# Local attention on other quarters of the array: scores with a head on each half of the partitions, values on all four quarters

## The chip, the cores and the metric

One core of a Trainium2 chip runs the whole program. The metric is the device time of one execution in microseconds (us). Engines are named as in the profile: PE is TensorE's matrix products, PEld its weight loads, DVE is VectorE, ACT is ScalarE, POOL is GpSimd, SP is SyncE, which issues the DMAs here.

## The reference, cut to what matters

```python
def sm_attn(qq, kk, vv):                          # softmax attention
    s = scale * np.matmul(qq, kk.transpose(0, 1, 3, 2))
    s = s - np.max(s, axis=-1, keepdims=True)
    a = np.exp(s)
    a = a / (np.sum(a, axis=-1, keepdims=True) + 1e-09)
    return np.matmul(a, vv)
q_d, k_d, v_d = means of q, k, v over groups of 4 tokens
out_up = np.repeat(sm_attn(q_d, k_d, v_d), 4, axis=2)
mask = np.abs(pos[:, None] - pos[None, :]) < 4    # local attention, 7 keys wide
out_local = softmax attention over the masked scores
x = (out_up + out_local)                          # (4608 tokens, 512)
h = x @ w_in                                      # 512 -> 2048
g = np.where(h >= 1, h, np.where(h <= -1, 0, (h + 1) ** 2 / 4))
return g @ w_out                                  # 2048 -> 512, float32
```

Here q, k and v are 8 batches x 8 heads x 576 tokens x 64 numbers, float32.

## The kernel before, in words

Two heads make a pair: with 64 numbers a head, a pair fills the 128 partitions, head h on the half that begins at 64 h. There are 32 pairs (8 batches of 4), and each goes through `attention` in ten pieces. The attention's output goes into a ring of two batches (`xh`, `xl`: two float32r parts whose sum is the number), and the feed-forward takes 12 chunks of 384 tokens from it, in steps of 128 hidden columns: `mm1` (L387, tile h_ps, then L398 to L404) and `mm2` (L425, tile o_ps).

Local attention cuts the 576 tokens into ten windows of 64 tokens, numbered i = 0 to 9, and computes 64 x 64 scores in each. A product with 64 rows and 64 columns of weights takes a quarter of TensorE's 128 x 128 array. Which quarter is set by its operands: the half of the partitions that they lie on is the row half, and the half of the partitions that the output lies on is the column half. I write a quarter as (row half, column half).

- **Scores (L146, tile sl_ps, 20 products a pair).** Operands are on the half of head h. Windows go two to a group, i = 2g + r, and the output is on half r, in PSUM bank h. For each g the products go to quarters (0,0), (1,1), (1,0), (0,1): all four in turn.
- **Softmax (L163 to L194)** works along a row, over a tile `sl` of 128 x 640. L163 adds the band mask and copies from PSUM to `sl`, through a view with the dimensions h, g, column.
- **Transposes (L213, tile tl_ps, 5 a pair)** of 128 x 128 each: after them (`al`, L217) the partitions are head and key, the columns are window half r and query.
- **Products with the values (L240, tile pl_ps, 20 a pair).** For window i and head h both operands lie on half h, and so does the output: quarters (0,0) and (1,1) alone, in turn. A product's columns are 53 to 61 output tokens. Output goes to PSUM bank 0 for windows 0 to 4 and bank 1 for 5 to 9, for either head.

Every one of these products is in float32, and shows as two passes in the trace: two weight loads and two matmuls, so a pair's 20 products are 40 matmul rows.

Beside these stand the pooled attention (sp_ps L156, tp_ps L222, pp_ps L252) and the sum of both (x, L263).

What sets the order: a scheduler places the instructions from the order in which the program gives them; each engine then runs its own list in that order. The first twelve pairs' pieces and the conversion of the weights from float64 (L298 to L309, on ACT, DVE and POOL) are placed by two written lists (`BEFORE_STEPS`, `FIRST_STEPS`). From the 49th step of the feed-forward on, `attn_step` spreads a pair over four steps, in pieces of 6, 0, 2 and 2, and `mm2` comes two steps behind `mm1`.

Of the kernel before, what the change touches and what calls it, by code (L numbers as in the profile page):

```python
# [17 lines left out]
P = 128  # L18
B, H, S, D = 8, 8, 576, 64
NPAIR = H // 2  # L20
# [12 lines left out]
RING = 2 * S  # L33
# Local attention runs on ten windows of 64 tokens: window start, first output
# token, number of output tokens.
WIN = 64
WIN_START = [0, 58, 116, 174, 232, 285, 343, 401, 459, 512]
OUT_START = [0, 61, 119, 177, 235, 288, 346, 404, 462, 520]
OUT_LEN = [61, 58, 58, 58, 53, 58, 58, 58, 58, 56]
NB = len(WIN_START)  # L40
NG = NB // 2
QB = 48
NQB = SD // QB
KB = 72
NKB = SD // KB
MASKED = -1.0e30
# Products at the very start, on operands that need no load, that take TensorE out of
# its slow clock.
WARM = 10
# The order in which the start's work is given to the scheduler, before the steps of the  # L50
# feed-forward and among the first of them. qN and v: loads of the first batch's
# operands, aN: the next of pair N's ten pieces, w: loads of the next weights, c: the
# conversion of the next unit of weights, s: the next step's product with w_in and its
# activation, m: the next step's product with w_out.
BEFORE_STEPS = """
# [14 lines left out]
class Rotation:  # L70
    """Tiles from several pools in turn."""

# [8 lines left out]
def attention_then_ffn(ctx: ExitStack, tc, qT, kT, vw, vp, band, w_in, w_out, out):  # L81
    nc = tc.nc
# [21 lines left out]
    def load(n, name):  # L104
        """The operand `name` of pair n, into the place that pair n - 1 has read."""
        if n == len(pairs):
            return
        b, p = pairs[n]
        if name == "q" or name == "k":
            t = apool.tile([P, S], F32, name=f"{name}_sb", tag=name, bufs=1)  # L110
            nc.sync.dma_start(t, (qT if name == "q" else kT)[b, p])
        elif name == "vp":
            t = apool.tile([KB, NKB, FACTOR, P], F32, name="vp_sb", tag="vp", bufs=1)
            nc.sync.dma_start(t, vp[b, p].rearrange("k (n f c) -> k n f c", n=NKB, f=FACTOR))
        else:
            t = apool.tile([P, NB, D], F32, name="v_sb", tag="v", bufs=1)
            nc.sync.dma_start(t, vw[b, p].rearrange("k (n d) -> k n d", n=NB))
        loaded[name] = t
# [4 lines left out]
    def attention(n, pool_1, pool_2):  # L123
        """One pair of heads, in ten pieces."""
        b, p = pairs[n]
        q, k = qk[p] if b == 0 else (loaded["q"], loaded["k"])
        M = 2 * QB
        # Sums over the groups of four tokens; the means' factors go into the
        # exponent's scale and into the output's.
        qd = apool.tile([P, SD], F32, name="qd", tag="qd", bufs=1)  # L130
# [8 lines left out]
        yield  # L139
        # Scores.  # L140
        sl_ps = pool_2.tile([P, 2, 512], F32, name="sl_ps", tag="a2")
        for g in range(NG):
            for r, h in ((0, 0), (1, 1), (0, 1), (1, 0)):
                w = WIN_START[2 * g + r]
                hs = slice(h * D, (h + 1) * D)
                nc.tensor.matmul(  # L146
                    sl_ps[r * WIN : (r + 1) * WIN, h, g * WIN : (g + 1) * WIN],
                    q[hs, w : w + WIN],
                    k[hs, w : w + WIN],
                    start=True,  # L150
                    stop=True,
                )
        sp_ps = pool_1.tile([P, 512], F32, name="sp_ps", tag="a1")
# [3 lines left out]
        if n + 1 >= NPAIR:  # L157
            load(n + 1, "q")
            load(n + 1, "k")
        yield  # L160
        # Local softmax, up to the exponential.
        sl = apool.tile([P, NG, 2, WIN], F32, name="sl", tag="sl", bufs=2)
        nc.vector.tensor_tensor(  # L163
            sl.rearrange("p g h c -> p h g c"),
            sl_ps[:, :, 0 : NG * WIN].rearrange("p h (g c) -> p h g c", c=WIN),
            band_sb.unsqueeze(1).unsqueeze(1).broadcast_to([P, 2, NG, WIN]),
            op=ALU.add,
        )
        slf = sl.rearrange("p g h c -> p (g h) c")
        ml = small(NB, "mxl")  # L170
# [5 lines left out]
        yield  # L176
        # Pooled softmax, up to the sums.
        sp = apool.tile([P, NQB, SD], F32, name="sp", tag="sp", bufs=1)
# [21 lines left out]
        for i in range(NQB):  # L200
            nc.scalar.mul(sp[:M, i], sp[:M, i], sm[:M, i : i + 1])
        # Sums of the values.
        vh = apool.tile([KB, NKB, 2, P], F32, name="vh", tag="al", bufs=1)
# [8 lines left out]
        for g in range(NG):  # L212
            nc.tensor.transpose(  # L213
                tl_v[:, g * P : (g + 1) * P], sl[:, g].rearrange("p h c -> p (h c)"), ident
            )
# [15 lines left out]
        v = loaded["v"]  # L231
        HS = S // 2
        for i in range(NB):
            g, r = divmod(i, 2)
            o = OUT_START[i]
            half = o // HS
            c0 = r * WIN + o - WIN_START[i]
            for h in range(2):
                hs = slice(h * D, (h + 1) * D)
                nc.tensor.matmul(  # L240
                    pl_ps[hs, half, o - half * HS : o - half * HS + OUT_LEN[i]],
                    v[hs, i, :],
                    al[hs, g, c0 : c0 + OUT_LEN[i]],
                    start=True,
                    stop=True,
                )
# [29 lines left out]

    # A unit of weights is a block of 128 hidden columns of w_in, or of rows of
    # w_out, raw at first, then in its place as two float32r parts.
    raw, weights = {}, {}
# [10 lines left out]
    def convert_weights(name, f):  # L290
        """float64 to the nearest float32, and that exactly into two float32r."""
        t = raw.pop((name, f))
        tf = t.bitcast(F32)
        m = temp("m")
        mi = m.bitcast(I32)
        # Eight of the high word's exponent bits come to lie under three zeros, with the
        # sign as the lowest of these, and then in a float32's place.
        nc.scalar.activation(m, tf[:, :, 1], AF.Copy, scale=2.0**-112)  # L298
        nc.vector.scalar_tensor_tensor(m, m, -(2.0**32), m, op0=ALU.mult, op1=ALU.max)  # L299
        nc.vector.tensor_scalar(mi, mi, 3, None, op0=ALU.logical_shift_left)  # L300
        # The low word, times the power of two and the sign of the high one.
        nc.vector.tensor_scalar(t[:, :, 1], mi, 0xFF800000 - (1 << 32), None, op0=ALU.bitwise_and)  # L302
        nc.vector.scalar_tensor_tensor(  # L303
            tf[:, :, 0], t.bitcast(U32)[:, :, 0], 2.0**-52, tf[:, :, 1], op0=ALU.mult, op1=ALU.mult
        )
        nc.vector.tensor_tensor(m, m, tf[:, :, 0], op=ALU.add)  # L306
        w = wpool.tile([P, 2, 512], F32R, name=f"w_{name}{f}", tag=f"w{name}{f}")
        nc.scalar.copy(w[:, 0], m)
        nc.gpsimd.tensor_tensor(w[:, 1], m, w[:, 0], op=ALU.subtract)  # L309
        weights[name, f] = w  # L310

# [1 line left out]
    # The first batch's queries and keys wait in the place of the last weights.  # L313
    qk = [
# [45 lines left out]

# [1 line left out]
    ps_h = ctx.enter_context(tc.tile_pool(name="ps_h", bufs=2, space=bass.MemoryType.PSUM))  # L362
# [3 lines left out]
    def attn_step(last):  # L366
        """Goes on with the attention of pairs under `last`, each over four steps."""
        if later["it"] is None:
            if later["n"] >= min(last, len(pairs)):
                return  # L370
            later.update(it=attention(later["n"], ps_a1, ps_a2), pieces=iter((6, 0, 2, 2)))
        for _ in range(next(later["pieces"])):
            if next(later["it"], later) is later:
                later.update(n=later["n"] + 1, it=None)
# [4 lines left out]
    def mm1(c, f):  # L379
# [15 lines left out]
        with tc.high_priority(offset=100):  # L395
            u = temp("u")[:, :TCH]
            # The square of relu((h + 1) / 2) is over h from 1 on.
            nc.scalar.activation(u, h[:, :TCH], AF.Relu, bias=0.5, scale=0.5)  # L398
# [41 lines left out]

    # The first half of the weights serves three chunks before the second has to
    # be there; the sums of two of them wait in DRAM.
    partial = dpool.tile([P, len(SPLIT), NTT, DM], F32, name="partial")
# [6 lines left out]
    for c, f in todo["s"]:  # L450
        # Batches whose places in the ring have been read, when this chunk runs.
        j, m = divmod(c, 3)
        attn_step(NPAIR * (2 * j + (2 if m < 2 else 3)))
        mm1(c, f)
        mm2(*next(todo["m"]))
# [50 lines left out]
```

## Time and profile before

| | |
|---|---|
| time, three runs | 1035.48, 1034.60 and 1034.48 us; median 1034.6 |
| span of the profiled execution, first to last instruction | 1033.2 us |
| what lies around the span (median less span) | 1.4 us |
| PE busy | 983.2 us, 95% |
| DVE, ACT, POOL busy | 445.4, 518.9, 409.3 us |
| mean granted TensorE clock | 0.974 of full speed |
| values' products (L240) | 1280 matmul rows, 47.9 us with at least one under way |
| scores' products (L146) | 1280 matmul rows, 29.2 us with at least one under way |

The profiled execution's own time isn't listed apart from its span; the median of the three runs stands for it, and 1.4 us is the difference. A row's duration for a matmul runs from its start to the modelled end of its output, so rows overlap: the distance from one start to the next tells the pace, not the duration.

### The profile page before, as it was taken

The page shows a single profiled execution, that of the slowest core. Times are in us where ns is not written, and L with a number is a line of the kernel's source. Part 1 is how long each engine was busy: PE and PEld are TensorE (multiplying, and loading weights), DVE is VectorE, ACT ScalarE, POOL GpSimd, SP SyncE. Part 2 cuts the span into 40 slices and gives each one's busy share as a digit, 9 for nine tenths or more (in the row PEclk, how much of TensorE's full clock was granted, in tenths as well). Part 3 has the DMA queues.
Part 4 walks back from the last instruction along what each step waited for, and adds up shares of the span by engine and source line. Part 5 has one row for each costly group of instructions (what it writes and reads, how often), then busy time and mean ns, then how long its engine had stood idle before and what let it go on. Part 6 is the DMA issues. An engine that isn't in the chain of part 4 may idle for free.

```text
span 1033.2 us, 18400 instructions
## 1 busy us (share of the span) xinstructions
PE 983.2 (95%) x7412; PEld 866.8 (84%) x7412; DVE 445.4 (43%) x774; ACT 518.9 (50%) x1189; POOL 409.3 (40%) x359
## 2 busy tenths in 40 slices
PE   5578798999999999999999999999999999999998
PEld 4466677889988888999888888899888888899997
DVE  7999979753254533113334443111443344111111
ACT  5456564545455554434555565433655555533433
POOL 3556555452245434322434444322443444322221
PEclk8579899999999999999999999999999999999999
DMA  7666410000133211100212311100311320000000
GB/s 265 206 232 212 152 56 1 32 23 31 44 117 109 92 49 53 50 1 24 79 48 72 101 49 48 56 1 3 99 49 48 93 62 34 31 1 1 31 1 31
DMA packets 28261, 69.37 MB, mean 67 GB/s; under 512 B 3344, under 2 KB 3344, under 8 KB 28176
## 3 DMA queue, kind: packets, MB, share of 16 engines
q1 hardware_dynamic: 28176, 68.20, 20.1%
q8 instruction: 58, 0.95, 0.4%
q14 instruction: 27, 0.22, 0.1%
HBM read 57.18 MB, written 11.01 MB: 66 GB/s over the span
## 4 chain that ended last, share of the span: by engine, by line
PE 80%; DVE 13%; issue 3%; ACT 2%; POOL 1%; DMA 1%; SPq 0%; DVEq 0%; ACTq 0%; POOLq 0%
PE h_ps L387 35%; PE o_ps L425 33%; PE pl_ps L240 3%; PE sp_ps L156 2%; DVE m L299 2%; PE tl_ps L213 2%; PE sl_ps L146 2%; PE pp_ps L252 2%; DVE m L306 1%; PE tp_ps L222 1%; DVE raw_o L303 1%; DVE raw_i L303 1%; DVE raw_i L302 1%; DVE m L300 1%; DVE u L400 1%
## 5 line engine op out<-in xcount | busy, mean ns | idle before, releaser
L387 PE MATMUL h_ps<-xh,w_i 128*128 128x384 f32 x1536 | 403.2, 344 | 9.8 <-DVE u L400 5.1
L404 POOL TENSOR_TENSOR gl<-u,gh 128x384 fp32r<-128x384 f32 x192 | 208.4, 1085 | 479.7 <-ACT gh L403 373.8
L425 PE MATMUL o_ps<-w_o,gh 128*128 128x512 f32 x1152 | 358.6, 392 | 0.7 <-ACT osb L435 0.6
L387 PEld LDWEIGHTS h_ps<-xh,w_i 128*128 128x128 f32 x1536 | 277.1, 190 | 26.2 <-DVE u L400 7.1
L400 DVE SCALAR_TENSOR_TENSOR u<-h_ps,u 128x384 f32<-128x384 f32 x192 | 106.6, 556 | 434.6 <-ACT u L399 408.2
L387 PE MATMUL h_ps<-xl,w_i 128*128 128x384 f32 x768 | 261.3, 341 | 0.9 <-POOL xl L273 0.9
L425 PEld LDWEIGHTS o_ps<-w_o,gh 128*128 128x128 f32 x1152 | 213.2, 188 | 35.2 <-ACT osb L435 2.2
L425 PE MATMUL o_ps<-w_o,gl 128*128 128x512 f32 x576 | 226.1, 393 | 1.3 <-POOL gl L404 1.3
L398 ACT ACTIVATE u<-h_ps 128x384 f32<-128x384 f32 x192 | 94.1, 491 | 175.5 <-PE h_ps L387 168.2
L403 ACT CAST gh<-u 128x384 fp32r<-128x384 f32 x192 | 98.5, 513 | 104.6 <-DVE u L400 103.2
L387 PEld LDWEIGHTS h_ps<-xl,w_i 128*128 128x128 f32 x768 | 145.5, 190 | 2.1 <-POOL xl L273 1.7
L425 PEld LDWEIGHTS o_ps<-w_o,gl 128*128 128x128 f32 x576 | 108.1, 188 | 25.5 <-POOL gl L404 2.8
L399 ACT ACTIVATE u<-u 128x384 f32<-128x384 f32 x192 | 100.3, 523 | 4.8
L185 ACT ACTIVATE sp<-sp_ps,mxp 96x144 f32<-96x144 f32 x96 | 35.1, 369 | 60.4 <-DVE mxp L183 59.3
L172 POOL TENSOR_TENSOR sl<-sl,mxl 128x640 f32<-128x640 f32 x32 | 41.2, 1289 | 55.3 <-DVE mxp L183 40.1
L273 POOL TENSOR_TENSOR xl<-x,xh 128x576 fp32r<-128x576 f32 x32 | 47.0, 1468 | 17.1 <-ACT xh L272 17.1
L240 PEld LDWEIGHTS pl_ps<-al,v_sb 64*64 64x64 f32 x1280 | 43.7, 145 | 11.0 <-issue 7.6
L205 POOL TENSOR_TENSOR vh<-vp_sb 72x512 f32<-72x512 f32 x32 | 42.6, 1331 | 23.1 <-PE pl_ps L240 10.3
L263 DVE TENSOR_TENSOR x<-pl_ps,xd 128x576 f32<-128x576 f32 x32 | 24.2, 755 | 60.3 <-ACT xd L261 57.9
L240 PE MATMUL pl_ps<-al,v_sb 64*64 64x58 f32 (+3 forms) x1280 | 47.9, 232 | 0.3 <-ACT ap L228 0.3
L156 PE MATMUL sp_ps<-kd,q_bd 128*96 128x144 f32 x192 | 34.9, 324 | 7.2 <-DVE kd L138 6.9
L213 PE MATMUL tl_ps<-ident,sl 128*128 128x128 f32 x160 | 25.7, 295 | 15.2 <-DVE sl L194 9.2
(59 smaller groups left out, 836.5 us busy)
## 6 DMA issues: line engine op xcount, KB each, us to landing
v_sb<-vw SPq DMA_DIRECT2D x32, 320.0 KB
vp_sb<-vp SPq DMA_DIRECT2D x32, 288.0 KB
raw_i<-w_in SPq DMA_DIRECT2D x16, 512.0 KB
raw_o<-w_out SPq DMA_DIRECT2D x16, 512.0 KB
q_sb<-qT SPq DMA_DIRECT2D x28, 288.0 KB
k_sb<-kT SPq DMA_DIRECT2D x28, 288.0 KB
out<-osb SPq DMA_DIRECT2D x30, 256.0 KB
partial<-osb SPq DMA_DIRECT2D x6, 256.0 KB
```

The source lines that it names most:

```text
L156: nc.tensor.matmul(sp_v[:, i, :], q_bd[:, i, :], kd, start=True, stop=True)
L205: nc.gpsimd.tensor_tensor(vh, vpt[:, :, 0:2, :], vpt[:, :, 2:4, :], op=ALU.add)
L213: nc.tensor.transpose(tl_v[:, g * P : (g + 1) * P], sl[:, g].rearrange("p h c -> p (h c)"), ident)
L240: nc.tensor.matmul(pl_ps[hs, half, o - half * HS : o - half * HS + OUT_LEN[i]], v[hs, i, :], al[hs, g, c0 : c0 + OUT_LEN[i]], start=True, ...
L273: nc.gpsimd.tensor_tensor(xl[:, p, r0 : r0 + S], x, xh[:, p, r0 : r0 + S], op=ALU.subtract)
L387: nc.tensor.matmul(h[:, :TCH], wi[:, wt, cc * P : (cc + 1) * P], xt[:, cc, ts], start=(n == 0), stop=(n == 3 * NCC - 1),)
L398: nc.scalar.activation(u, h[:, :TCH], AF.Relu, bias=0.5, scale=0.5)
L399: nc.scalar.activation(u, u, AF.Square)
L400: nc.vector.scalar_tensor_tensor(u, h[:, :TCH], 1.0, u, op0=ALU.max, op1=ALU.min)
L403: nc.scalar.copy(gh, u)
L404: nc.gpsimd.tensor_tensor(gl, u, gh, op=ALU.subtract)
L425: nc.tensor.matmul(o, gt[:, ts], wo[:, wt, :], start=starts and n == 0, stop=ends and n == 2)
```

## The change

The quarters are dealt out anew. For the scores, the output's half no longer is the window's r. It is `place(h, g)`: head h's own half for groups 0 to 2, the other half for groups 3 and 4. A group now is the windows g and g + 5 (i = r * 5 + g), and the order is written out in `SCORE_ORDER`. Groups 0 to 2 lie in bank 0 and groups 3 and 4 in bank 1, side by side (columns 128 to 767 of the two banks), so L163 reads and writes one stretch of 640. After the transposes the partitions are window half r and key, the columns are head place and query. So the values' products have their operands on half r and their output on half h: quarters (0,0), (1,1), (1,0), (0,1) in turn, with the output in bank r. The values are laid out to match on the host (same bytes, same row length). The rest of the diff blanks comments.

```diff
+BANK = 3
+SL0 = 512 - BANK * 2 * WIN
+def place(h, g):
+    return h if g < BANK else 1 - h
+SCORE_ORDER = [
+    (h, r, g)
+    for gs in ((0, 3), (1, 4), (2,))
+    for r in range(2)
+    for g in gs
+    for h in (range(2) if g < BANK else (1, 0))
+]
...
         sl_ps = pool_2.tile([P, 2, 512], F32, name="sl_ps", tag="a2")
-        for g in range(NG):
-            for r, h in ((0, 0), (1, 1), (0, 1), (1, 0)):
-                w = WIN_START[2 * g + r]
-                hs = slice(h * D, (h + 1) * D)
-                nc.tensor.matmul(
-                    sl_ps[r * WIN : (r + 1) * WIN, h, g * WIN : (g + 1) * WIN],
...
+        sl_v = sl_ps.rearrange("p a c -> p (a c)")[:, SL0 : SL0 + NB * WIN]
+        for h, r, g in SCORE_ORDER:
+            w = WIN_START[r * NG + g]
+            hs = slice(h * D, (h + 1) * D)
+            x, c = place(h, g), (2 * g + r) * WIN
+            nc.tensor.matmul(
+                sl_v[x * WIN : (x + 1) * WIN, c : c + WIN],
+                q[hs, w : w + WIN],
+                k[hs, w : w + WIN],
...
+        slf = sl.rearrange("p g r c -> p (g r) c")
         nc.vector.tensor_tensor(
-            sl.rearrange("p g h c -> p h g c"),
-            sl_ps[:, :, 0 : NG * WIN].rearrange("p h (g c) -> p h g c", c=WIN),
-            band_sb.unsqueeze(1).unsqueeze(1).broadcast_to([P, 2, NG, WIN]),
+            slf,
+            sl_v.rearrange("p (n c) -> p n c", c=WIN),
+            band_sb.unsqueeze(1).broadcast_to([P, NB, WIN]),
             op=ALU.add,
         )
...
-        for i in range(NB):
-            g, r = divmod(i, 2)
-            o = OUT_START[i]
-            half = o // HS
-            c0 = r * WIN + o - WIN_START[i]
-            for h in range(2):
+        for g in range(NG):
+            for r, h in ((0, 0), (1, 1), (1, 0), (0, 1)):
                 hs = slice(h * D, (h + 1) * D)
+                rs = slice(r * WIN, (r + 1) * WIN)
+                i = r * NG + g
+                o = OUT_START[i]
+                c0 = place(h, g) * WIN + o - WIN_START[i]
                 nc.tensor.matmul(
-                    pl_ps[hs, half, o - half * HS : o - half * HS + OUT_LEN[i]],
-                    v[hs, i, :],
-                    al[hs, g, c0 : c0 + OUT_LEN[i]],
+                    pl_ps[hs, r, o - r * HS : o - r * HS + OUT_LEN[i]],
+                    v[rs, 2 * g + h, :],
+                    al[rs, g, c0 : c0 + OUT_LEN[i]],
```

On PE, the values' products of the last pair, and what stands beside them, before the change:

```order
L425 MATMUL o_ps_8357<-w_o_1965,gl 128x512
L240 MATMUL pl_ps<-al,v_sb 64x61 x2
L240 MATMUL pl_ps<-al,v_sb 64x58 x6
L240 MATMUL pl_ps<-al,v_sb 64x53 x2
L240 MATMUL pl_ps<-al,v_sb 64x58 x8
L240 MATMUL pl_ps<-al,v_sb 64x56 x2
L252 MATMUL pp_ps<-ap,vd 64x144 x4
L387 MATMUL h_ps<-xh,w_i_2157 128x384 x2
```

The same place with the change (lines are numbered anew: L261 is the values' product, L273 the pooled one, L408 and L446 the feed-forward's):

```order
L446 MATMUL o_ps_8357<-w_o_1965,gl 128x512
L261 MATMUL pl_ps<-al,v_sb 64x61
L261 MATMUL pl_ps<-al,v_sb 64x58 x2
L261 MATMUL pl_ps<-al,v_sb 64x61
L261 MATMUL pl_ps<-al,v_sb 64x58 x12
L261 MATMUL pl_ps<-al,v_sb 64x53
L261 MATMUL pl_ps<-al,v_sb 64x56 x2
L261 MATMUL pl_ps<-al,v_sb 64x53
L273 MATMUL pp_ps<-ap,vd 64x144 x4
L408 MATMUL h_ps<-xh,w_i_2157 128x384 x2
```

The window with 61 tokens and the one with 58 now come in turn, which is window 0 beside window 5; there are 20 products as before, at the same place in PE's list. Apart from these blocks PE's list is the same, and so are the lists of ACT, POOL and SP; in DVE's list L163 alone has another shape. On PE, the scores of the last pair before the change:

```order
L425 MATMUL o_ps_8357<-w_o_1658,gl 128x512
L146 MATMUL sl_ps<-k_sb,q_sb 64x64 x20
L156 MATMUL sp_ps<-kd,q_bd 96x144 x3
L387 MATMUL h_ps<-xh,w_i_1853 128x384 x2
```

And with it:

```order
L446 MATMUL o_ps_8357<-w_o_1658,gl 128x512
L166 MATMUL sl_ps<-k_sb,q_sb 64x64 x20
L176 MATMUL sp_ps<-kd,q_bd 96x144 x3
L408 MATMUL h_ps<-xh,w_i_1853 128x384 x2
```

Nothing moved here: what differs, the quarter of each of the 20, isn't in these rows. It follows from the code.

## Rows read from the trace of the kernel before

**Rows 1.** The page's first lines: span, busy time of each engine.
```profile
span 1033.2 us, 18400 instructions
PE 983.2 (95%) x7412; PEld 866.8 (84%) x7412; DVE 445.4 (43%) x774; ACT 518.9 (50%) x1189; POOL 409.3 (40%) x359
```

**Rows 2.** Busy time by stage: stretch, length, busy us (x) by engine, clock, DMA.
```profile
40.00:60.00 20.00, 11.22 (x127) 9.51 (x128) 20.00 (x34) 10.71 (x26) 10.14 (x8) 0.59 0.62 203
100.00:120.00 20.00, 13.71 (x98) 11.50 (x96) 20.00 (x28) 8.62 (x18) 10.48 (x10) 0.83 0.56 194
230.00:290.00 60.00, 60.00 (x387) 54.26 (x386) 20.68 (x42) 31.07 (x74) 19.59 (x18) 1.00 0.12 39
345.00:1033.00 688.00, 684.60 (x5026) 609.54 (x5024) 200.82 (x389) 331.84 (x755) 242.58 (x219) 1.00 0.14 44
```

**Rows 3.** The page's chain that ended last, shares of the span by engine.
```profile
PE 80%; DVE 13%; issue 3%; ACT 2%; POOL 1%; DMA 1%; SPq 0%; DVEq 0%; ACTq 0%; POOLq 0%
```

**Rows 4.** Timeline, last pair: start, length, engine, line, operation, tiles, shape, count.
```profile
871.66 0.81 PE L146 MATMUL sl_ps<-k_sb,q_sb 64*64 64x64 f32 x40
872.41 0.98 PE L156 MATMUL sp_ps<-kd,q_bd 128*96 128x144 f32 x6
...
886.90 1.37 PE L240 MATMUL pl_ps<-al,v_sb 64*64 64x61 f32 x40
888.20 0.71 PE L252 MATMUL pp_ps<-ap,vd 72*64 72x144 f32 x8
```

**Rows 5.** Timeline of PE, the first 0.1 us of the values' block.
```profile
886.90 0.27 PE L240 MATMUL pl_ps<-al,v_sb 64*64 64x61 f32 x2
```

**Rows 6.** PE busy from a block's first start to the next block's: values, then scores.
```profile
42.35:44.61 2.26, 2.26 (x41) 0.53 0.25 84
87.34:88.61 1.27, 1.27 (x41) 0.50 0.00 0
```

**Rows 7.** Timeline of PE where the third pair's values and fourth pair's scores meet.
```profile
35.32 0.37 PE L146 MATMUL sl_ps<-first_o,first_i 64*64 64x64 f32 x2
35.41 0.32 PE L240 MATMUL pl_ps<-al,v_sb 64*64 64x56 f32 x2
```

**Rows 8.** Values' tile alone by stage: busy us (x) of PE, PEld, DVE.
```profile
280.00:345.00 65.00, 5.50 (x160) 4.98 (x160) 3.03 (x4) 1.00 0.35 111
345.00:660.00 315.00, 16.50 (x480) 14.93 (x480) 9.10 (x12) 1.00 0.17 53
660.00:1033.00 373.00, 11.00 (x320) 9.95 (x320) 6.06 (x8) 1.00 0.11 36
```

**Rows 9.** Scores' tile alone by stage, same columns.
```profile
0.00:60.00 60.00, 6.48 (x200) 5.51 (x200) 4.02 (x5) 0.70 0.68 229
60.00:140.00 80.00, 3.65 (x146) 3.04 (x146) 2.44 (x3) 0.90 0.53 180
140.00:280.00 140.00, 1.27 (x54) 0.99 (x54) 1.64 (x2) 0.99 0.08 28
280.00:345.00 65.00, 2.44 (x120) 2.02 (x120) 2.46 (x3) 1.00 0.35 111
```

**Rows 10.** The chain that ended last, in order of time: two pieces of the start.
```profile
33.41 2.21 PE pl_ps L240 x38
...
131.58 1.30 PE pl_ps L240 x40
```

**Rows 11.** Timeline of DVE, the sum that waits for the first of these.
```profile
35.87 0.76 DVE L263 TENSOR_TENSOR x<-pl_ps,xd 128x576 f32<-128x576 f32 x1 [1.76 <-PE pl_ps L240]
```

**Rows 12.** Line 163: duration of one in ns, minimum, median and maximum.
```profile
L163 DVE TENSOR_TENSOR sl<-sl_ps,band_sb x32: 785/825/826, 6.8 to 872.5; 128x640 f32<-128x640 f32 x32
```

**Rows 13.** Timeline: last inputs of the last pair's values, and of the step behind.
```profile
883.71 0.64 ACT L228 COPY ap<-tp_ps 72x576 f32<-72x576 f32 x1 [0.78 <-PE tp_ps L222]
...
887.34 1.00 POOL L404 TENSOR_TENSOR gl<-u,gh 128x384 fp32r<-128x384 f32 x1 [4.36 <-issue]
```

More of the change, by code (lines that the diff above doesn't have):

```diff
@@ L141, in attention @@
         sl_ps = pool_2.tile([P, 2, 512], F32, name="sl_ps", tag="a2")
-        for g in range(NG):
-            for r, h in ((0, 0), (1, 1), (0, 1), (1, 0)):
-                w = WIN_START[2 * g + r]
-                hs = slice(h * D, (h + 1) * D)
-                nc.tensor.matmul(
-                    sl_ps[r * WIN : (r + 1) * WIN, h, g * WIN : (g + 1) * WIN],
[L148 to L152, printed above, removed]
+        sl_v = sl_ps.rearrange("p a c -> p (a c)")[:, SL0 : SL0 + NB * WIN]
[7 more added lines that the diff above has]
+                k[hs, w : w + WIN],
+                start=True,
+                stop=True,
+            )
         sp_ps = pool_1.tile([P, 512], F32, name="sp_ps", tag="a1")
@@ L162, in attention @@
         sl = apool.tile([P, NG, 2, WIN], F32, name="sl", tag="sl", bufs=2)
+        slf = sl.rearrange("p g r c -> p (g r) c")
         nc.vector.tensor_tensor(
-            sl.rearrange("p g h c -> p h g c"),
-            sl_ps[:, :, 0 : NG * WIN].rearrange("p h (g c) -> p h g c", c=WIN),
-            band_sb.unsqueeze(1).unsqueeze(1).broadcast_to([P, 2, NG, WIN]),
+            slf,
+            sl_v.rearrange("p (n c) -> p n c", c=WIN),
+            band_sb.unsqueeze(1).broadcast_to([P, NB, WIN]),
             op=ALU.add,
         )
-        slf = sl.rearrange("p g h c -> p (g h) c")
         ml = small(NB, "mxl")
@@ L213, in attention @@
             nc.tensor.transpose(
-                tl_v[:, g * P : (g + 1) * P], sl[:, g].rearrange("p h c -> p (h c)"), ident
+                tl_v[:, g * P : (g + 1) * P], sl[:, g].rearrange("p r c -> p (r c)"), ident
             )
@@ L475, in words @@
         return np.ascontiguousarray(a).view(np.int64)
-    windows = np.stack([v[:, :, w : w + WIN, :] for w in WIN_START], axis=3)
+    windows = np.stack([v[:, :, w : w + WIN, :] for w in WIN_START], axis=2)
+    windows = windows.reshape(B, NPAIR, 2, 2, NG, WIN, D).transpose(0, 1, 3, 5, 4, 2, 6)
     windows = np.ascontiguousarray(windows).reshape(B, NPAIR, 2 * WIN, NB * D)
```

## The prediction

> **What bounds the kernel now.** I read the page's busy line first, then the busy time by stage, then the chain that ended last, then the timeline of one pair. The busy line has PE at 983.2 of 1033.2 us and nothing else above 50% [rows 1]. The stages show that this is an average over two regimes [rows 2]. In 40 to 60 and in 100 to 120 DVE is busy 20.00 of 20 us, and PE only 11.22 and 13.71: the weights' conversion and the first pairs' softmax hold the start, on DVE. From 230 on PE has no gap (60.00 of 60), and from 345 to the end it is busy 684.60 of 688.00 at the full clock. The chain says the same: 80% PE, 13% DVE [rows 3]. So a nanosecond saved on PE behind some 200 us comes off the end, and one saved ahead of that mostly doesn't.
>
> **The values' products.** In the last pair the scores' block starts at 871.66 and what follows it starts at 872.41: 0.75 us for 40 passes. The values' block starts at 886.90, its follower at 888.20: 1.30 us, also for 40 passes [rows 4]. The scores go round four quarters, so each quarter holds 10 passes; the values go round two, so each holds 20. Ten passes more in a quarter cost 0.55 us, 0.055 us a pass, with 0.20 us around them (0.75 - 10 x 0.055). That reading needs the quarters to run side by side, each at its own pace. The first 0.1 us of the values' block shows two passes that together span 0.27 us [rows 5], so (0,0) and (1,1) start together. Better still, at 35.32 two passes of the scores start ahead of the last two of the values at 35.41 [rows 7], though PE's list has all 20 values' products first: the scores' third and fourth product lie in the two quarters that the values leave empty, and didn't have to wait.
>
> With the change the values have 10 passes in each of four quarters, the same quarters in the same turn as the scores before, and with each row half writing a bank of its own, as the scores did. Their block should take 0.75 us: 0.55 us less a pair. A product streams 53 to 61 columns against the scores' 64. I take nothing for that; at most a tenth of the 0.55 could come on top, which is 0.05 us a pair.
>
> **The scores' products.** The first 16 of `SCORE_ORDER` still go (0,0), (1,1), (1,0), (0,1). The last four, of group 2, go (0,0), (1,1), (0,0), (1,1). So (0,0) and (1,1) hold six products, 12 passes, and the other two hold 8. The block ends with the fuller quarters: two passes more, 2 x 0.055 = 0.11 us dearer, 0.86 in place of 0.75.
>
> **How many pairs count.** From 280 to the end the values' tile has 160 + 480 + 320 = 960 passes [rows 8], 24 of the 32 pairs, all in the regime without gaps. The scores of these 24 pairs start from 135 on. The earliest is split, and its tail, which is what grows, lies at 227: of the 54 passes in 140 to 280, 40 are a whole block and 14 are that tail [rows 9]. So 24 pairs on both sides: 24 x (-0.55) = -13.2, 24 x 0.11 = +2.6, together **-10.6 us**.
>
> Is something else late there once PE is faster? The values' last input (ap) is ready at 884.35, 2.55 us ahead of their start at 886.90. The low part of the activation (gl) of the step at hand ends at 888.34 [rows 13], and PE takes it two steps later. A shift by 0.55 eats into neither.
>
> **The start.** Eight pairs' values and about as many score blocks lie ahead of 140 us, where DVE is the limit. At the half clock a values' block takes 2.26 us and a scores' block 1.27 [rows 6], so a block there gains up to 0.99, and the scores lose 2 x 0.099 = 0.20. Two values' blocks are on the chain [rows 10]. At 35.87 DVE had sat idle for 1.76 us until the values ended [rows 11], so nearly the whole 0.99 can come off there; at 131.58 it is 0.55. I take 1.3 of these 1.5 us, since other work on DVE's list soon is as late. Bounds: if every one of the eight counted, four at each clock, 4 x 0.99 + 4 x 0.55 = 6.2 us gained; if only the scores' tails counted, 4 x 0.20 + 4 x 0.11 = 1.2 us lost.
>
> **L163** keeps its 640 elements and loses a dimension of its view. It took 785 to 826 ns [rows 12]; no row shows the flat form. I take no change. A few hundredths either way on the twelve pairs in the DVE-bound start are 0.5 us at most; later DVE waits for PE. The loads of v keep bytes and row length: nothing.
>
> **Sum.** 1033.2 - 10.6 - 1.3 = 1021.3 us of span. The three runs' median stands 1.4 above the profiled span, and I leave that as it is: **1022.7 us**, 1.2% faster.
>
> **Rivals.**
>
> *The shared bank (slower).* In the new scores both row halves write bank 0 for groups 0 to 2 (12 products) and bank 1 for groups 3 and 4 (8 products); before, each row half had a bank to itself. If a bank served one row half at a time, bank 0's 24 passes would come one after the other: 0.20 + 24 x 0.055 = 1.52 us a block, 0.77 more than before. Against the 0.55 won on the values that is +0.22 a pair, 24 x 0.22 = +5.3: 1039.9 us, with nothing gained in the start. It turns at a scores' block of 1.30 us; any longer and the change loses. The Trainium skill, "TensorEngine Tiling (Array Packing)", Gotcha 1, states that different row tiles cannot access the same PSUM bank simultaneously; read as a wait, that is this rival. What speaks against it is that the values before already write one bank from both row halves, window by window, and their two passes start together [rows 5]. By that row the halves of the partitions don't disturb each other. 5%.
>
> *The scores give it back (no change).* If the new turn of the scores ran two quarters at a time as the values do, their block would grow from 0.75 to 1.30 and cancel the gain: about 1033.3 with the start's 1.3. For it: the last four products do run so. Against: the first 16 keep the old turn exactly. 6%.
>
> *The start pays in full (more).* The gain ahead of 140 us is nearer its bound of 6.2 than 1.3, since each PE block that ends sooner lets DVE's list go on: 1034.6 - 10.6 - 6.2 = 1017.8. For it: the 1.76 us that DVE waits [rows 11]. Against: DVE busy 20.00 of 20. 6%.
>
> **How the numbers follow.** My forecast has 83%. Its own range is the start's bounds, cut to the likely part, and a few hundredths a pair: 1018.5 to 1026. To hold 8 in 10 I widen it a little on both sides, to 1017.5 to 1027, which takes in the full start. Runs of this kernel differ by a tenth of a per cent, so 0.2% (2.1 us) is what can be told from no change. Faster: 83 + 6 and a little of the second rival, 90%. Within 0.2%: 5%. Slower: the shared bank, 5%.
>
> **What would show it.** Right: a values' block 0.75 us long from its first start to the pooled products', in all 24 late pairs; a scores' block of 0.86; the distance from one pair's scores to the next shorter by 0.44 us; no new wait of PE behind 345. Wrong: scores of 1.3 us or more (a bank's turn), values still at 1.30 (quarters not independent, or a bound common to all four), or blocks as predicted and PE idle in their place.

## The result, and the profile after

The changed kernel takes 1022.93 us (median of 4, 1022.67 to 1023.42) against 1034.54 before (median of 4, one run more than in the table above): ratio 0.9892, interval 0.988 to 0.9904. That is 11.6 us or 1.1% faster; 1022.7 was forecast. A second set of runs gave 1022.56, ratio 0.9887 (0.9874 to 0.9901).

The page's first lines after, which answer to [rows 1]:

```profile
span 1021.6 us, 18401 instructions
PE 968.0 (95%) x7412; PEld 851.1 (83%) x7412; DVE 444.4 (44%) x774; ACT 518.7 (51%) x1189; POOL 410.7 (40%) x359
```

PE is busy 15.2 us less, with as many instructions; the span is 11.6 us shorter. So some 3.6 us of what PE saved came back as idle time: 2.6 of it ahead of 280 us, in these two traces, and 1.0 between 280 and 345. The other engines' sums are the same to within 1.4 us.

The timeline of PE after, at the last two pairs (answers to [rows 4]; start, length, engine, line, operation, tiles, shape, count):

```profile
854.84 0.80 PE L261 MATMUL pl_ps<-al,v_sb 64*64 64x61 f32 x40
855.57 0.71 PE L273 MATMUL pp_ps<-ap,vd 72*64 72x144 f32 x8
...
860.55 0.92 PE L166 MATMUL sl_ps<-k_sb,q_sb 64*64 64x64 f32 x40
861.39 0.98 PE L176 MATMUL sp_ps<-kd,q_bd 128*96 128x144 f32 x6
...
875.89 0.80 PE L261 MATMUL pl_ps<-al,v_sb 64*64 64x61 f32 x40
876.62 0.71 PE L273 MATMUL pp_ps<-ap,vd 72*64 72x144 f32 x8
```

Read it from start to start. The values' block is 875.89 to 876.62, 0.73 us where it was 1.30. The scores' block is 860.55 to 861.39, 0.84 where it was 0.75. The 24 late values' blocks are all 0.73 long but one: pair 9's, whose followers had to wait, as is shown below. From one pair's values to the next it is 875.89 - 854.84 = 21.05 us. Before, the last block started at 886.90 [rows 4], and the one ahead of it here:

```profile
865.38 1.38 PE L240 MATMUL pl_ps<-al,v_sb 64*64 64x61 f32 x40
```

That was 886.90 - 865.38 = 21.52 us, so a late pair is 0.47 us cheaper.

The stretch of the last pieces that the two written lists place, pairs 8 to 11, reads otherwise. Busy time of PE, PEld, DVE, ACT and POOL from 280 to 345 us, before:

```profile
280.00:345.00 65.00, 64.33 (x611) 55.86 (x610) 29.84 (x58) 36.87 (x95) 29.13 (x26) 1.00 0.35 111
```

and after, with the stage behind it:

```profile
280.00:345.00 65.00, 63.34 (x653) 54.26 (x651) 30.19 (x59) 36.90 (x95) 29.20 (x27) 1.00 0.36 111
345.00:1021.00 676.00, 673.01 (x4978) 598.55 (x4974) 200.45 (x388) 331.30 (x754) 240.20 (x219) 1.00 0.14 44
```

PE's idle time in the first stretch grew from 0.67 to 1.66 us; behind 345 it is 3.0 of 676, as before (3.4 of 688 in [rows 2]). The waits themselves stand in brackets at the end of a row of the timeline. Between 285 and 330 us PE had two before:

```profile
292.10 0.95 PE L156 MATMUL sp_ps<-kd,q_bd 128*96 128x144 f32 x6 [0.23 <-DVE kd L138]
310.00 0.76 PE L213 MATMUL tl_ps<-ident,sl 128*128 128x128 f32 x5 [0.32 <-DVE sl L163]
```

and has five after:

```profile
289.46 0.92 PE L166 MATMUL sl_ps<-k_sb,q_sb 64*64 64x64 f32 x40 [0.20 <-DVE x L284]
290.81 0.95 PE L176 MATMUL sp_ps<-kd,q_bd 128*96 128x144 f32 x6 [0.43 <-DVE kd L157]
303.38 0.71 PE L273 MATMUL pp_ps<-ap,vd 72*64 72x144 f32 x8 [0.18 <-ACT sp L205]
308.40 0.77 PE L233 MATMUL tl_ps<-ident,sl 128*128 128x128 f32 x5 [0.17 <-DVE sl L184]
317.25 0.77 PE L233 MATMUL tl_ps<-ident,sl 128*128 128x128 f32 x5 [0.68 <-DVE x L284]
```

0.55 us of waits became 1.66, so 1.11 us are new. L163, now L184 with its flat view, takes what it took [rows 12]:

```profile
L184 DVE TENSOR_TENSOR sl<-sl_ps,band_sb x32: 786/825/826, 7.1 to 861.5; 128x640 f32<-128x640 f32 x32
```

### The profile page after: what moved, and what is told of

Same layout as the page of the kernel before. It is cut to its first block, busy times and chain, and to the rows that moved or that the text cites. A ratio compares the mean times of both kernels' runs of the same rounds, so it can differ in the third digit from the quotient of the medians.

```text
span 1021.6 us, 18401 instructions
## 1 busy us (share of the span) xinstructions
PE 968.0 (95%) x7412; PEld 851.1 (83%) x7412; DVE 444.4 (44%) x774; ACT 518.7 (51%) x1189; POOL 410.7 (40%) x359
## 4 chain that ended last, share of the span: by engine, by line
PE 79%; DVE 12%; issue 3%; ACT 3%; POOL 1%; DMA 1%; SPq 0%; DVEq 0%; ACTq 0%; POOLq 0%
PE h_ps L408 35%; PE o_ps L446 34%; PE sp_ps L176 2%; PE sl_ps L166 2%; DVE m L320 2%; PE pl_ps L261 2%; PE pp_ps L273 2%; PE tl_ps L233 2%; PE tp_ps L242 1%; DVE m L327 1%; DVE raw_o L324 1%; DVE raw_i L324 1%; DVE u L421 1%; DVE raw_o L323 1%; DVE m L321 1%
## 5 line engine op out<-in xcount | busy, mean ns | idle before, releaser
L408 PE MATMUL h_ps<-xh,w_i 128*128 128x384 f32 x1536 | 403.4, 344 | 7.5 <-DVE u L421 5.2
L446 PE MATMUL o_ps<-w_o,gh 128*128 128x512 f32 x1152 | 358.4, 392 | 1.6 <-ACT gh L424 1.6
L408 PEld LDWEIGHTS h_ps<-xh,w_i 128*128 128x128 f32 x1536 | 277.7, 190 | 24.2 <-DVE u L421 7.1
L408 PE MATMUL h_ps<-xl,w_i 128*128 128x384 f32 x768 | 261.8, 341 | 2.7 <-POOL xl L294 2.7
L446 PEld LDWEIGHTS o_ps<-w_o,gh 128*128 128x128 f32 x1152 | 213.2, 188 | 35.7 <-ACT gh L424 2.5
L446 PE MATMUL o_ps<-w_o,gl 128*128 128x512 f32 x576 | 226.4, 393 | 1.3 <-POOL gl L425 1.3
L408 PEld LDWEIGHTS h_ps<-xl,w_i 128*128 128x128 f32 x768 | 145.9, 190 | 3.8 <-POOL xl L294 3.4
L446 PEld LDWEIGHTS o_ps<-w_o,gl 128*128 128x128 f32 x576 | 108.3, 188 | 25.7 <-POOL gl L425 2.9
L225 POOL TENSOR_TENSOR vh<-vp_sb 72x512 f32<-72x512 f32 x32 | 45.5, 1422 | 16.7 <-DMA vp_sb<-vp 5.8
L233 PEld LDWEIGHTS tl_ps<-ident,sl 128*128 128x128 f32 x160 | 20.2, 150 | 23.3 <-DVE x L284 7.0
L184 DVE TENSOR_TENSOR sl<-sl_ps,band_sb 128x640 f32<-128x640 f32 x32 | 26.2, 820 | 28.5 <-PE sl_ps L166 28.5
```

Of the source, the lines that this page charges most:

```text
L225: nc.gpsimd.tensor_tensor(vh, vpt[:, :, 0:2, :], vpt[:, :, 2:4, :], op=ALU.add)
L233: nc.tensor.transpose(tl_v[:, g * P : (g + 1) * P], sl[:, g].rearrange("p r c -> p (r c)"), ident)
L408: nc.tensor.matmul(h[:, :TCH], wi[:, wt, cc * P : (cc + 1) * P], xt[:, cc, ts], start=(n == 0), stop=(n == 3 * NCC - 1),)
L446: nc.tensor.matmul(o, gt[:, ts], wo[:, wt, :], start=starts and n == 0, stop=ends and n == 2)
```

## The experiments

Three questions were open. Is it the quarters that made the values faster, or the banks, since the change altered both? Does the scores' 0.09 come from the fuller quarters? And which pairs brought the 11.6 us? In the experiments' diffs, the minus lines are the changed kernel.

**Values back on two quarters, with separate banks.** The product's output goes to the half of its row, so only (0,0) and (1,1) work; the products that start together write different banks.

```diff
-                    pl_ps[hs, r, o - r * HS : o - r * HS + OUT_LEN[i]],
+                    pl_ps[rs, h, o - r * HS : o - r * HS + OUT_LEN[i]],
```

> The changed kernel with the values' output put on the half of the window's row (quarters (0,0) and (1,1) alone again), head h in bank h; the heads' outputs land on the wrong halves, the work is the same. Theory (each quarter runs its own passes at 0.055 us): a values' block is 1.30 us again, the scores' block stays at 0.845, so a late pair is 0.10 dearer than before the change: some 1037 us. Rival (what slowed the values was both row halves writing one bank): here the two products that start together write different banks, so the block is 0.73 as with the change, and the time about 1023.

Measured: 1036.46 us, ratio to before 1.0021 (1.0012 to 1.0029). PE's timeline of this kernel, last pair:

```profile
872.29 0.91 PE L166 MATMUL sl_ps<-k_sb,q_sb 64*64 64x64 f32 x40
873.13 0.98 PE L176 MATMUL sp_ps<-kd,q_bd 128*96 128x144 f32 x6
...
887.63 1.37 PE L261 MATMUL pl_ps<-al,v_sb 64*64 64x61 f32 x40
888.93 0.71 PE L273 MATMUL pp_ps<-ap,vd 72*64 72x144 f32 x8
```

The values' block is 1.30 again, with the new scores still at 0.84. So separate banks alone gain nothing, and the gain comes with the four quarters. That four quarters need no separate banks is shown for the scores alone, in the next experiment. What is left is the price of the new scores by itself: 0.2%, some 2 us.

**Scores dealt evenly.** The swap of places comes after the fifth of ten score blocks (2g + r below 5), not after the third group; each quarter has five products.

```diff
-BANK = 3
-SL0 = 512 - BANK * 2 * WIN
+SL0 = 512 - NG * WIN
-def place(h, g):
-    return h if g < BANK else 1 - h
+def place(h, g, r):
+    return h if 2 * g + r < NG else 1 - h
 SCORE_ORDER = [
-    (h, r, g)
-    for gs in ((0, 3), (1, 4), (2,))
-    for r in range(2)
-    for g in gs
-    for h in (range(2) if g < BANK else (1, 0))
+    (h, n % 2, n // 2)
+    for j in range(NG)
+    for n in (j, j + NG)
+    for h in (range(2) if n < NG else (1, 0))
 ]
...
```

> The changed kernel with the scores dealt five to each quarter: the head's place swaps at the sixth of ten score blocks, not between groups, five blocks in each bank. Theory (the scores' block ends with its fullest quarter): 10 passes in place of 12, a block of 0.742 in place of 0.845 us, -0.10 for each of 20 late pairs, some 0.3 for pairs 8 to 11 and up to 0.5 in the start: 1020.4 us, with 1020.0 to 1020.9 likely. Rival (the 0.10 comes from both row halves writing one bank): it stays at 0.845 and at 1022.9 us.

Measured: 1021.93 us (4 runs, 1019.89 to 1022.87), ratio 0.9875 (0.986 to 0.989). The block did what the theory says, in PE's timeline of this kernel:

```profile
860.12 0.81 PE L163 MATMUL sl_ps<-k_sb,q_sb 64*64 64x64 f32 x40
860.86 0.98 PE L173 MATMUL sp_ps<-kd,q_bd 128*96 128x144 f32 x6
```

0.74 us, within 0.01 of the block before the change [rows 4], though both row halves still share the banks. The time missed its forecast by 1.5 us. So it was run again, beside the changed kernel on the same chip.

> The scores dealt five to each quarter once more, beside the changed kernel on the same chip. Theory: 2.1 us off in the 20 late pairs (0.103 each) and up to 0.5 elsewhere, 1020.4 to 1020.9. Rival (what it gains late it loses in the start, as its first profile hinted): 1022 or more.

> The changed kernel once more, beside the next three on one chip: 1022.9 us. The profiles so far differ by 1 to 3 us in the first 140 us even where that stretch's program is the same, so single profiles don't decide a microsecond of the start.

Measured: 1020.71 us (ratio 0.9865, 0.9852 to 0.9879) for the even scores, 1022.56 us (0.9887, 0.9874 to 0.9901) for the changed kernel. The medians differ by 1.0 us in the first pair of runs and 1.85 in the second, the same way both times. On the one chip no run of the even scores took over 1021.06 us, and none of the changed kernel under 1022.44, so the rival (1022 or more) fell. The intervals of the two ratios overlap, so how much of the 2.1 us arrives isn't settled by the times. The traces settle it for the late pairs. Pair 12's scores start, in the changed kernel and with the even scores, at

```profile
328.35 0.91 PE L166 MATMUL sl_ps<-k_sb,q_sb 64*64 64x64 f32 x40
```

```profile
329.96 0.75 PE L163 MATMUL sl_ps<-k_sb,q_sb 64*64 64x64 f32 x36
```

From there to the last pair's scores, at 860.55 and 860.12, it is 532.20 and 530.16 us: 2.04 us in 19 pairs, 0.11 each. At pair 12 the profiled execution of the even scores, the slowest of its set at 1022.87 us, was 1.6 us behind the changed kernel's; in the second set the two were level there (328.18 and 328.15). This is the best version here: it beats both kernels at the median in both sets.

**Values in another order.** First the ten products of (0,0) and (1,1), then the ten of the other two quarters.

```diff
-        for g in range(NG):
-            for r, h in ((0, 0), (1, 1), (1, 0), (0, 1)):
+        for two in (((0, 0), (1, 1)), ((1, 0), (0, 1))):
+            for g, (r, h) in itertools.product(range(NG), two):
```

> The changed kernel with the values' 20 products in another order: first the ten of quarters (0,0) and (1,1), then the ten of (1,0) and (0,1). Theory (a product waits only for its own quarter, and PE looks far enough ahead): a block of 0.73 to 0.80 us and about 1023 us. Rival (products start in the order of PE's list, so the turn decides): 1.30 us, as with two quarters, and about 1036 us. Between the two: PE looks ahead only some way.

Measured: 1031.46 us, ratio 0.9974 (0.9964 to 0.9984). Neither end came out:

```profile
884.22 1.20 PE L261 MATMUL pl_ps<-al,v_sb 64*64 64x61 f32 x40
885.34 0.71 PE L273 MATMUL pp_ps<-ap,vd 72*64 72x144 f32 x8
```

1.12 us: 0.18 less than the 1.30 of strict order, which is three passes in a quarter. PE's busy time from the block's start to 884.62, values' tile alone, with the passes in brackets:

```profile
884.20:884.62 0.42, 0.40 (x14) 1.00 0.00 0
```

By then 14 of the first ten products' 20 passes had started, and the next to start were the third and fourth quarter's first. Of the values' passes under way between 884.60 and 884.63, one is of 61 columns, and long like a block's first (264 ns): it is window 0 in quarter (0,1).

```profile
L261 PE MATMUL pl_ps<-al,v_sb x11: 218/218/264, 884.4 to 884.6; 64*64 64x58 f32 x10, 64*64 64x61 f32 x1
```

So six of the first ten's passes were still to start. PE does start passes ahead of others in its list, but only some way. If that reach is about six passes, turning by fours should do nearly as well as turning by twos.

```diff
-        for g in range(NG):
-            for r, h in ((0, 0), (1, 1), (1, 0), (0, 1)):
+        for gs in ((0, 1), (2, 3), (4,)):
+            for two, g, n2 in itertools.product((0, 1), gs, (0, 1)):
+                r, h = (((0, 0), (1, 1)), ((1, 0), (0, 1)))[two][n2]
```

> The changed kernel with the values' products turned by two groups: four products in quarters (0,0) and (1,1), then four in (1,0) and (0,1), and so on. Theory (PE starts a pass up to six passes ahead of what still waits, as read from the order with ten and ten, where the third quarter started with six passes left): a block of 0.73 to 0.80 us. Rival (the third quarter started early there only because the first ten ran out): some 1.1 us as with ten and ten.

Measured in its profile (a single run, 1023.76 us):

```profile
876.17 0.84 PE L262 MATMUL pl_ps<-al,v_sb 64*64 64x61 f32 x40
876.95 0.71 PE L274 MATMUL pp_ps<-ap,vd 72*64 72x144 f32 x8
```

0.78 us, within the theory's range. The values' tile alone at the block's start, again with the passes in brackets:

```profile
876.16:876.20 0.04, 0.03 (x2) 1.00 0.00 0
```

Two of the first four products' eight passes had started when the third quarter's first one did, at 876.20. So six were still to start, as with ten and ten, and the rival fell: the third quarter doesn't wait until the products ahead run out. The turn matters, then, at the scale of a few products.

**Which pairs pay.** Three kernels hold both versions of scores, mask and values, and choose by the pair's number n; the values' layout follows on the host. For pairs 12 on:

```diff
-        for h, r, g in SCORE_ORDER:
+        for h, r, g in SCORE_ORDER if n >= FIRST else ():
...
+        for g in range(NG) if n < FIRST else ():
+            for r, h in ((0, 0), (1, 1), (0, 1), (1, 0)):
...
+    windows[: FIRST // NPAIR] = first[: FIRST // NPAIR]
```

with FIRST = 12, then 8; and the reverse, the new version for pairs 0 to 7 alone.

> Pairs 0 to 11 as before the change, pairs 12 to 31 as changed. Theory (20 late pairs give 0.47 us each, the rest of the 11.6 comes from earlier): 1034.5 - 9.4 = 1025.1 us. Rival (the first twelve pairs give nothing, since they lie where DVE is the limit, and the late ones give 0.57 each): 1023.1 us.

> Pairs 0 to 7 as before the change, pairs 8 to 31 as changed. Theory (pairs 8 to 11 lose half their gain to new waits of PE for DVE and ACT, about 0.8 us in all come of them): 1034.5 - 9.4 - 0.8 = 1024.3 us. Rival (all 24 late pairs pay in full, 0.47 each): 1034.5 - 11.3 = 1023.2 us.

> Pairs 0 to 7 as changed, pairs 8 to 31 as before. The prediction's start term: 1.3 us gained, 1033.2. What the kernels with late pairs alone leave over (11.6 less 10.9): 0.7 us, 1033.8. Rival (the start gains nothing, DVE being the limit): 1034.5, no change.

| new version for | measured us | ratio to before (interval) | gain us |
|---|---|---|---|
| pairs 12 to 31 | 1024.72 | 0.9906 (0.9892 to 0.992) | 9.8 |
| pairs 8 to 31 | 1023.75 | 0.9898 (0.9882 to 0.9915) | 10.9 |
| pairs 0 to 7 | 1033.27 | 0.9991 (0.9982 to 1.0) | 1.0 |
| all | 1022.93 | 0.9892 (0.988 to 0.9904) | 11.6 |

Pairs 12 to 31 alone came out near the theory's 1025.1, and the rival's 1023.1 lies just outside the interval. Pairs 8 to 31 fell midway between 1024.3 and 1023.2, so the time decides nothing there. Pairs 0 to 7 gained about what either estimate says, with no gain at the interval's edge. The parts add up: 10.9 + 1.0 = 11.9 against 11.6. With pairs 0 to 11 as before, PE's waits between 285 and 330 us are those of before:

```profile
290.94 0.95 PE L188 MATMUL sp_ps<-kd,q_bd 128*96 128x144 f32 x6 [0.23 <-DVE kd L158]
308.85 0.76 PE L253 MATMUL tl_ps<-ident,sl 128*128 128x128 f32 x5 [0.32 <-DVE sl L204]
```

With pairs 8 to 11 changed as well, and the start still as before, all five waits of the changed kernel are back; the longest:

```profile
317.52 0.77 PE L253 MATMUL tl_ps<-ident,sl 128*128 128x128 f32 x5 [0.68 <-DVE x L318]
```

So these waits come of the change in pairs 8 to 11 itself. By the times alone, pairs 8 to 11 take the gain from 9.8 to 10.9: about 1 us, with an interval wider than that. By the traces it is told apart better: the start of pair 8's values and of pair 12's scores, before the change,

```profile
287.30 1.38 PE L240 MATMUL pl_ps<-al,v_sb 64*64 64x61 f32 x40
...
330.54 0.81 PE L146 MATMUL sl_ps<-k_sb,q_sb 64*64 64x64 f32 x40
```

and with pairs 8 to 31 new:

```profile
286.31 0.80 PE L295 MATMUL pl_ps<-al,v_sb 64*64 64x61 f32 x40
...
328.61 0.92 PE L167 MATMUL sl_ps<-k_sb,q_sb 64*64 64x64 f32 x40
```

The first starts 0.99 us earlier, the second 1.93: 0.94 us. That stretch holds the four pairs' values, but the scores of pairs 10 and 11 only. The dearer scores of pairs 8 and 9 lie ahead of it, from the second part of pair 8's block on. It starts, before the change, with pairs 8 to 31 new, and with all pairs new, at

```profile
227.47 0.46 PE L146 MATMUL sl_ps<-k_sb,q_sb 64*64 64x64 f32 x14
```

```profile
226.30 0.56 PE L167 MATMUL sl_ps<-k_sb,q_sb 64*64 64x64 f32 x14
```

```profile
225.99 0.56 PE L166 MATMUL sl_ps<-k_sb,q_sb 64*64 64x64 f32 x14
```

From there to pair 12's scores it is 103.07 us before, 102.31 with pairs 8 to 31 new, and 102.36 with all new (328.35, above). So the four pairs give 0.76 us (0.71 in the last), where 4 x 0.47 would be 1.9; the 1.11 us of new waits make the difference.

## Why the prediction was right

**The mechanism held.** A pair's 20 products of a kind end with the quarter that holds most passes, where the turn between quarters is short. The sizes came out a little off the 0.055 us a pass: the values gained 0.57, not 0.55 (ten passes at 0.057), the scores lost 0.09 to 0.10, not 0.11. Together a late pair gives 0.47 where 0.44 was forecast. The 58 columns against 64, for which I took nothing and at most 0.05, are worth at most 0.02: the new values' block of ten passes is 0.73 against the scores' 0.74 to 0.75.

**"24 pairs on both sides, all in the regime without gaps" was wrong for four of them.** In 280 to 345 the written list interleaves two pairs at close quarters. Shorter products bring PE sooner to instructions whose inputs come from DVE or ACT: the sum x, the reduction kd, the pooled softmax. The slack that I showed was that of the last pair, where `attn_step` leaves a step or more between pieces, and I carried it back to pairs 8 to 11, where there is none. They gave 0.76 us, not the 1.8 of the sum. The 20 pairs behind them gave 20 x 0.47 = 9.4, not 8.8. The two errors partly cancel: 10.2 against 10.6. That the total came as near as 0.3 us is in part luck, of these two errors and of a start that is known no better than below.

**The start** was put at 1.3 us with bounds of 6.2 gained and 1.2 lost. Alone it measured 1.0 us, with an interval from 0 to 1.9. The size can't be told better than that, and no trace shows it by itself, because the start shifts between executions by as much. The kernel with pairs 12 to 31 changed runs the first 280 us as before, and still its pair 8's values start at 286.14, 1.16 us earlier than in the trace of before:

```profile
286.14 1.38 PE L281 MATMUL pl_ps<-al,v_sb 64*64 64x61 f32 x40
```

One source can be seen, the first load's landing, in the first scores' row of before, of the even scores and of the kernel with pairs 0 to 7 new:

```profile
5.43 1.35 PE L146 MATMUL sl_ps<-first_o,first_i 64*64 64x64 f32 x40 [5.43 <-DMA first_o<-kT]
```

```profile
6.65 1.35 PE L163 MATMUL sl_ps<-first_o,first_i 64*64 64x64 f32 x40 [6.65 <-DMA first_o<-kT]
```

```profile
4.91 1.54 PE L167 MATMUL sl_ps<-first_o,first_i 64*64 64x64 f32 x40 [4.91 <-DMA first_o<-kT]
```

The same load released PE anywhere from 4.9 to 6.7 us. So a reading of the start by one trace, as in my two blocks on the chain [rows 10], is worth no more than a microsecond or so.

**L163** at no change was right: 786/825/826 ns against 785/825/826.

**The rivals.** The shared bank fell: with both row halves writing one bank the scores' block is 0.84 at 12 passes and 0.74 at 10, what the fullest quarter alone gives; it would have been 1.52. The rule of the Trainium skill, "TensorEngine Tiling (Array Packing)", Gotcha 1, that different row tiles can't access one PSUM bank at the same time, isn't borne out as a wait by these rows, in which the two row tiles write different halves of the partitions. No run here has them write the same partitions of a bank. "The scores give it back" fell with the same rows: they gave back 0.10 of 0.57, not all. "The start pays in full" fell too: 1.0 and not 6.2.

## What to carry to other kernels

When a block of small products uses part of the array, count the passes in its fullest quarter: here the block ended with that one. A layout that puts work on the idle quarters pays by the passes that it takes from the fullest (0.057 us each here), and an uneven deal costs what its fullest quarter holds too much. Keep the turn between quarters short in program order; with ten products of two quarters in a row, most of the gain was lost. And take slack from the stage it is claimed for: PE without gaps in one stretch says nothing on how late its inputs are in the next.

## What the runs showed of the hardware

I had not expected how far PE starts passes out of its list's order, and where that ends; that each engine runs its own list in order, as I put it above, isn't exact for PE. With ten products a side, the third quarter started when six passes of the first two had not: a block of 1.12 us, between 0.73 and 1.30. With four a side it again started with six passes ahead of it unstarted, and the block is 0.78, 0.05 above the turn by twos. Both are at the full clock. At a granted clock of 0.50 (before the change, 35.20 to 35.60) the count is the same in [rows 7]: what starts at 35.32 has six passes ahead of it in PE's list, the two of the values at 35.41 and the four of the scores' first two products. All of this is for 64 x 64 weights, and what sets the reach isn't shown.
